# Gate logits with the tokens as the stationary operand: products turned around in a fused attention and mixture-of-experts kernel

## The chip, the cores and the metric

One core of one Trainium2 chip runs the whole program. The metric is device time in microseconds (us) of one execution. TensorE is called PE in the rows below (PEld are its weight loads), VectorE DVE, ScalarE ACT, GpSimd POOL, and SyncE, which issues most transfers, SP.

## The reference

Windowed attention with four sink positions runs over 4 batches and 8 heads of 768 positions with 64 channels; its output, laid out as 3072 tokens of 512 channels, goes through a mixture of 8 experts of which each token takes one. All arithmetic is in float32.

```python
scores = scale * np.matmul(q, k.transpose(0, 1, 3, 2))
keep = is_sink | in_window                      # 4 sinks, window of 128
scores = np.where(keep, scores, -1000000000.0)
a = np.exp(scores - np.max(scores, axis=-1, keepdims=True))
a = a / (np.sum(a, axis=-1, keepdims=True) + 1e-09)
x = np.matmul(a, v)                             # then tokens x 512 channels
logits = x @ w_gate                             # 512 x 8
e_idx = np.argmax(logits, axis=1)
gate_w = softmax(logits) at e_idx
eom = 1.0 / (1.0 + np.exp(-(x @ w_output_gate)))   # 512 x 8
out[mask] = gate_w * eom[:, e] * (np.maximum(x[mask] @ w1[e], 0.0) @ w2[e])
```

## The kernel before

**Attention by pairs.** Two neighbouring heads make a pair, `pair(p)` with p from 0 to 15, four pairs to a batch. For each of six blocks of 128 queries, PE forms the scores in 64x64 tiles (`score`, L1232) in a PSUM tile `s`, DVE folds the window and takes the maximum (`fold`, L1239 to L1244), and ACT takes the exponentials (`exps`, L1248) into `e`. There are two `s` tiles, so the third block of scores waits for the exponentials of the first. PE turns `e` over (`trans`, L1272), ACT copies that to `f` (L1275), POOL cuts the triangles (L367), and PE multiplies by the values in 64x64 tiles (`av`, L1335; the sinks in `av_sink`, L1357) into two PSUM tiles, `oA` for even blocks and `oB` for odd ones. Each exists once, so the next pair's first `av` waits until the last reader of this pair's `oA` and `oB` is done. ACT copies both to `ot` (L1363), which has channels on its partitions and tokens along its rows, not yet divided by the sums of the exponentials `rs`. `norm` (L1411, L1414) turns `ot` over, divides, and writes `x`, which is stored to `xd` in HBM.

**The gate, before.** `gate1` (L1370) holds the gate weights `wgt` (128 channels x 32: 16 columns for each head of the pair) as the stationary operand and streams the 128 tokens of a block past it, six products in 128x32 tiles; the logits come out with the 32 columns on partitions, in the fourth quarter of `oA` and `oB`. ACT copies them to `lgT` (L1375), PE turns them over with two transposes in a tile of the family `tp` (`gate2`, L1381; there are two `tp` tiles, which every turning shares), DVE multiplies by the reciprocals in `rs` (`weigh`, L1385) into `lw`, and POOL (DVE for the last two pairs) adds the heads into `lg` (L1393, L1395). After a batch's last pair, `gate_route` chooses each token's expert, counts (L546, L548) and sorts the tokens into a table: six PE products (`sort`, L610) and an addition on DVE (L613).

**The experts.** Four early slots (256 tokens of the commonest experts so far) can begin before attention ends; after the fourth batch's table, `final_table` splits what is left into 13 slots, each one expert's share of up to 384 tokens. A slot gathers its tokens (L890), turns them over (L950), splits them into a high part `xh` (ACT) and a low part `xl` (DVE, L955), and multiplies by both layers' weights (L1055 in the first early slot; L1074 and L1087, first layer; L1112, second layer), three products for each where the weights are split too. A half megabyte of weights is loaded into one of four `raw` tiles; ACT makes the high part (L925) and DVE the low part (L929, 1024 wide).

**What sets the order.** Nothing is written in the order in which it runs. Each step is given to a planner (`Plan.op`) with its engine, costs, tiles and a due time made of `AT` and `PAIR * p` (for a slot of `SLOT0 + STEP * k`), and for some steps overridden by `PIN`, a table by step number. `Plan.order` puts the steps of each engine in line, the engines then run in that order, and a step whose input is late holds up what stands behind it.

```python
pl.op("PE", fn=gate1, r=["wgt", (ot, 0), (ot, 1)], w=[oA, oB], at=(at, "g1"), **pe(450, "quad"))
pl.op("PE", fn=gate2, r=[(lgT, 0), (lgT, 1)], w=[gt], at=(at, "g2"), **pe(170))
pl.op("DVE", fn=weigh, r=[gt, (rs, "r")], w=[lw], at=(at, "lw"), **dve(192))
```

## Time and profile before

| what | value |
|---|---|
| median of 3 runs | 514.02 us (513.76 to 514.71) |
| profiled execution, its own time | 513.68 us |
| span of its instructions | 511.9 us |
| PE busy | 486.7 us (95%) |
| PE's weight loads busy | 384.0 us (75%) |
| DVE, ACT, POOL busy | 335.1, 285.0, 196.1 us |
| mean granted clock | 0.991 |

The span is what the instructions of the profiled execution cover; its own time is 1.8 us more. A PE that is busy in the rows is not one at its peak: products overlap, and the end of each is modelled. In the trace each float32 product stands as two records (six products of `gate1` are 12 records), so rows count records. All times in rows are from the start of the span.

### The profile page before, as it was taken

What the parts mean: (1) busy time and instruction counts of PE and PEld (TensorE: products, weight loads), DVE (VectorE), ACT (ScalarE), POOL (GpSimd) and SP (SyncE); (2) the same over time, 40 slices, a digit from 0 to 9 for tenths busy, and PEclk for the clock granted to TensorE, in tenths of its full rate; (3) what the DMA queues carried; (4) which work ended last, traced back from release to release, by engine and by line L of the source; (5) the groups of instructions that cost most, each with busy time, mean ns of one, the idle gap of its engine ahead of it and who ended that gap; (6) DMA issues with size and microseconds to landing.
All of it is one profiled execution on the core that took longest, in us unless ns stands there. A gap on an engine that the chain in (4) does not pass through costs nothing.

```text
span 511.9 us, 12956 instructions
## 1 busy us (share of the span) xinstructions
PE 486.7 (95%) x4797; PEld 384.0 (75%) x4797; DVE 335.1 (65%) x776; ACT 285.0 (56%) x773; POOL 196.1 (38%) x314
## 2 busy tenths in 40 slices
PE   8799989999999999999799999999999999999992
PEld 3467667766567884998799989989866878878872
DVE  4677897799856498899898621543636866275430
ACT  4788878878866525844446332534537856363430
POOL 7777778886882224231155023021133211000020
PEclk9999999999999999999899999999999999999997
DMA  8455653758961445974838449483898889986460
GB/s 302 128 168 153 216 161 124 233 166 297 388 187 40 155 131 201 315 258 146 294 101 314 148 153 343 156 293 90 282 363 319 283 289 310 367 266 230 141 260 21
DMA packets 61402, 112.52 MB, mean 220 GB/s; under 512 B 8076, under 2 KB 27664, under 8 KB 61330
## 3 DMA queue, kind: packets, MB, share of 16 engines
q1 hardware_dynamic: 56866, 97.47, 56.6%
q0 software_dynamic: 4464, 14.14, 7.9%
q8 instruction: 40, 0.66, 0.5%
q14 instruction: 32, 0.26, 0.1%
HBM read 98.41 MB, written 13.44 MB: 219 GB/s over the span
## 4 chain that ended last, share of the span: by engine, by line
PE 56%; issue 16%; DVE 12%; DMA 7%; ACT 5%; POOL 2%; another core or an unknown queue 0%; POOLq 0%; ACTq 0%; DVEq 0%
PE s L1074 14%; PE oA L1112 9%; PE oB L1112 7%; DMA raw<-in_w_dram 7%; PE s L1232 6%; PE tp L1272 3%; PE s L1055 3%; PE oA L1335 3%; PE oB L1335 2%; ACT e L1248 2%; PE tp L1411 2%; PE s L1087 2%; DVE nmx L1244 2%; DVE s L1241 1%; POOL out_dram L968 1%
## 5 line engine op out<-in xcount | busy, mean ns | idle before, releaser
L1248 ACT ACTIVATE e<-s,nmx 128x132 f32<-128x132 f32 x192 | 69.7, 371 | 28.5 <-DVE nmx L1244 24.6
L968 POOL DMA_INDIRECT out_dram<-y,idx x20 | 21.7, 1087 | 108.3 <-ACT y L965 94.4
L890 POOL DMA_INDIRECT xg<-xd,idx x21 | 24.5, 1168 | 93.3 <-PE tp L950 77.9
L986 ACT ACTIVATE hh<-s 128x512 fp32r<-128x512 f32 (+1 forms) x36 | 23.2, 644 | 64.3 <-PE s L1074 64.0
L1232 PE MATMUL s<-k,q 64*64 64x196 f32 (+1 forms) x768 | 51.8, 341 | 6.6 <-ACT e L1248 6.1
L989 DVE SCALAR_TENSOR_TENSOR hl<-s,hh 128x512 fp32r<-128x512 f32 (+1 forms) x36 | 26.8, 747 | 41.9 <-ACT hh L986 41.9
L1241 DVE COPY_PREDICATED s<-maskf,s 128x256 f32<-128x256 int32 x80 | 33.9, 424 | 15.9 <-PE s L1232 13.8
L1244 DVE TENSOR_REDUCE nmx<-s 128x2 f32<-128x264 f32 x96 | 41.5, 432 | 3.3
L1232 PEld LDWEIGHTS s<-k,q 64*64 64x64 f32 x768 | 23.3, 133 | 26.0 <-ACT e L1248 15.7
L1211 POOL TENSOR_SCALAR q<-q 128x256 f32<-128x256 f32 x45 | 37.9, 855 | 5.8 <-DMA q<-in_qT_dram 3.7
L1248 ACT ACTIVATION_READ_ACCUMULATOR e<-s,nmx 128x1 f32 x192 | 38.8, 202 | 0.0
L367 POOL TENSOR_SCALAR_AFFINE_SELECT g<-f 128x512 f32<-128x512 f32 (+1 forms) x48 | 27.6, 576 | 24.5 <-ACT f L1275 24.5
L1335 PE MATMUL oB<-g,v 64*64 64x128 f32 (+1 forms) x384 | 32.0, 248 | 0.2 <-ACT tick L1348 0.2
L1272 PE MATMUL tp<-ident,e 128*128 128x128 f32 x192 | 30.3, 282 | 1.7 <-DVE x L1414 0.8
L1275 ACT COPY f<-tp 128x512 f32<-128x512 f32 x48 | 28.1, 593 | 6.4 <-PE tp L1272 4.3
L1335 PE MATMUL oB<-f,v 64*64 64x64 f32 (+1 forms) x384 | 31.0, 244 | 0.0
L1335 PE MATMUL oA<-f,v 64*64 64x128 f32 (+1 forms) x384 | 30.6, 251 | 0.3 <-POOL f L367 0.3
L367 POOL TENSOR_SCALAR_AFFINE_SELECT f<-f 128x512 f32<-128x512 f32 (+1 forms) x48 | 27.0, 562 | 3.3
L1272 PEld LDWEIGHTS tp<-ident,e 128*128 128x128 f32 x192 | 20.8, 141 | 9.3 <-issue 2.4
L968 POOL DMA_INDIRECT out_dram<-y,idx_e x8 | 10.8, 1354 | 40.7 <-ACT y L965 39.4
L965 ACT ACTIVATE y<-oA,sc 128x512 f32<-128x512 f32 (+1 forms) x18 | 11.7, 651 | 23.6 <-PE oA L1112 18.0
L1335 PEld LDWEIGHTS oB<-g,v 64*64 64x64 f32 x384 | 23.0, 133 | 2.1 <-issue 1.0
(563 smaller groups left out, 1596.5 us busy)
## 6 DMA issues: line engine op xcount, KB each, us to landing
raw<-in_w_dram SPq DMA_DIRECT2D x96, 512.0 KB
v<-in_vx_dram SPq DMA_DIRECT2D x8, 768.0 KB
xd<-x SPq DMA_DIRECT2D x16, 384.0 KB
k<-in_kx_dram SPq DMA_DIRECT2D x15, 396.0 KB
q<-in_qT_dram SPq DMA_DIRECT2D x15, 384.0 KB
wa0h<-in_w_dram SPq DMA_DIRECT2D x2, 512.0 KB
wa0l<-in_w_dram SPq DMA_DIRECT2D x2, 512.0 KB
wa1h<-in_w_dram SPq DMA_DIRECT2D x2, 512.0 KB
```

The source lines that it names most:

```text
L367: nc.gpsimd.affine_select(out=ap, in_=ap if src is None else src, pattern=pattern, compare_op=op, fill=fill, base=base, channel_multiplier=cm)
L968: nc.gpsimd.indirect_dma_start(out=where, out_offset=bass.IndirectOffsetOnAxis(ap=ids(), axis=0), in_=p.get(yk)[:, 0:m], in_offset=None, b ...
L1074: nc.tensor.matmul(out=p.get(ps)[:, j, 0:cols], lhsT=a, rhs=p.get(x)[:, d, 0:cols], start=d == 0 and i == 0, stop=d == ND - 1 and i == 2)
L1112: nc.tensor.matmul(out=p.get(ys[s]), lhsT=h[a][:, s * P:(s + 1) * P], rhs=w[b_], start=f == 0 and i == 0, stop=f == NF - 1 and i == len(th ...
L1211: (nc.gpsimd if p else nc.vector).tensor_scalar(out=c, in0=c, scalar1=SCALE, scalar2=None, op0=ALU.mult)
L1232: nc.tensor.matmul(out=get(s)[h * D:(h + 1) * D, a, c0:c1], lhsT=get(q)[r, t * P + h * D:t * P + (h + 1) * D], rhs=get(k)[r, k0 + c0 - o0: ...
L1241: nc.vector.copy_predicated(out=both[:, :, 4:CW], mask=bc(maski[:, 1, 4:CW], 1, 2), data=z[:, :, 0:P])
L1244: nc.vector.tensor_reduce(out=get(nmx)[:, t, :], in_=both, axis=AX.X, op=ALU.max, negate=True)
L1248: nc.scalar.activation(out=get(e)[:, t, a, :], in_=get(s)[:, a, P:P + CW], func=AF.Exp, bias=get(nmx)[:, t, a:a + 1], scale=1.0, accum_out ...
L1272: nc.tensor.transpose(out=get(tp)[:, i, :], in_=get(e)[:, 2 * j + i // 2, i % 2, 4:CW], identity=ident)
L1275: nc.scalar.copy(out=get(f)[:, two].rearrange("p t a r -> p (t a) r"), in_=get(tp))
L1335: nc.tensor.matmul(out=o, lhsT=get(v)[rows_, kt, p % 2 * P + a * D:p % 2 * P + (a + 1) * D], rhs=get((f, g)[src == "g"])[rows_, kt, a, c0: ...
```

## The change

The gate's products are turned around. In `gate`, a 64x64 piece of `ot` (64 channels of one head x 64 tokens) is the stationary operand, and that head's 16 columns of `wgt` stream past it: 24 products for a pair (six blocks, two halves of the tokens, two heads), cycling through the four 64x64 tiles that the scores use. The logits come out with tokens on partitions, the even head's in `oA` and the odd head's in `oB`. The two ACT copies to `lgT` and the two transposes are gone, and with them one use of a `tp` tile. DVE weighs straight from `oA` and `oB`, in two instructions of 96 columns where there was one of 192; they, and no longer ACT, are the last readers of `oA` and `oB`. The planner's numbers (`SOFT`, `SLOT0`, `AT`, `PIN`) are new throughout, so all engines run in another order. The amount of work outside the gate is the same.

```diff
-SOFT = 12779
-SLOT0, STEP, PLAIN, FSTEP = 196777, 20000, 1, 800
+SOFT = 13716
+SLOT0, STEP, PLAIN, FSTEP = 196911, 20000, 1, 800
...
-    12: -24621, 50: 3844, 52: 25562, 59: -91499, 60: -90999, 61: -91498, 66: -14940, 68: 18874, 69: 19874, 71: 18872,
+    12: -24621, 18: 2353, 21: 1853, 24: 10220, 35: 64141, 36: 1854, 44: 4741, 50: 5428, 51: 64641, 52: 26563,
...
-            lgT = new(pl, "lgT", [96, 2, P], key=("lgT", p))
-
-            def gate1():
-                for i, o in enumerate((oA, oB)):
-                    for j in range(3):
-                        nc.tensor.matmul(out=get(o)[32 * j:32 * j + 32, 3, :], lhsT=wgt[:, hp, :], rhs=get(ot)[:, 3 * i + j, :],
-                                         start=True, stop=True, skip_group_check=True)
-
-            pl.op("PE", fn=gate1, r=["wgt", (ot, 0), (ot, 1)], w=[oA, oB], at=(at, "g1"), **pe(450, "quad"))
-            for i, o in enumerate((oA, oB)):
-                pl.op("ACT", fn=lambda i=i, o=o: nc.scalar.copy(out=get(lgT)[:, i, :], in_=get(o)[0:96, 3, :]), r=[o], w=[(lgT, i)], at=(at, "lgT"), **act(128))
-            gt, lw = new(pl, "tp", [P, 4, P]), new(pl, "lw", [P, T, 2, 2 * E])
-
-            def gate2():
-                lr = get(gt).rearrange("p a q -> p (a q)")[:, 0:2 * 96]
-                for a in range(2):
-                    nc.tensor.transpose(out=lr[:, a * 96:(a + 1) * 96], in_=get(lgT)[:, a, :], identity=ident[0:96, 0:96])
-
-            def weigh():
-                lr = get(gt).rearrange("p a q -> p (a q)")[:, 0:2 * 96]
-                tt(out=get(lw), in0=lr.rearrange("p (t a e) -> p t a e", t=T, a=2), in1=bc(get(rs), 3, 2 * E), op=ALU.mult)
+            def gate():
+                for t in range(T):
+                    for h in range(2):
+                        for a, o in enumerate((oA, oB)):
+                            r = slice(a * D, (a + 1) * D)
+                            nc.tensor.matmul(out=get(o)[h * D:(h + 1) * D, 3, t * 2 * E:(t + 1) * 2 * E], lhsT=get(ot)[r, t, h * D:(h + 1) * D],
+                                             rhs=wgt[r, hp, a * 2 * E:(a + 1) * 2 * E], start=True, stop=True, skip_group_check=True)
+
+            pl.op("PE", fn=gate, r=["wgt", (ot, 0), (ot, 1)], w=[oA, oB], at=(at, "g1"), **pe(550, "four"))
+            lw = new(pl, "lw", [P, T, 2, 2 * E])
+
+            def weigh(a, o):
+                def fn():
+                    tt(out=get(lw)[:, :, a, :], in0=get(o)[:, 3, 0:T * 2 * E].rearrange("p (t e) -> p t e", t=T),
+                       in1=bc(get(rs)[:, :, a], 2, 2 * E), op=ALU.mult)
+                return fn
...
-            pl.op("PE", fn=gate2, r=[(lgT, 0), (lgT, 1)], w=[gt], at=(at, "g2"), **pe(170))
-            pl.op("DVE", fn=weigh, r=[gt, (rs, "r")], w=[lw], at=(at, "lw"), **dve(192))
+                pl.op(name, fn=fn, r=[(lw, 0), (lw, 1)] if hp == 0 else [(lw, a)], w=[lg], at=(at, "add"), **cost)
+
+            for i, o in enumerate((oA, oB)):
+                pl.op("DVE", fn=weigh(i, o), r=[o, (rs, "r")], w=[(lw, i)], at=(at, "lw"), **dve(96))
```

The order of PE around the first pair's gate, before (tiles by their names, with numbers where there are several; the last column is the shape of the output and how many equal products follow each other; line numbers of after are 17 higher around the attention):

```order
L1303 MATMUL tp_555<-ident,pk_541 24x128 x2
L1370 MATMUL oA<-ot_545,wgt 32x128 x3
L1370 MATMUL oB<-ot_545,wgt 32x128 x3
L1411 MATMUL tp_573<-ident,ot_545 128x128 x4
L1411 MATMUL tp_578<-ident,ot_545 128x128 x2
L1232 MATMUL s_212<-k_234,q_229 64x196 x4
L1232 MATMUL s_209<-k_234,q_229 64x196 x4
L1381 MATMUL tp_604<-ident,lgT_592 128x96 x2
L1272 MATMUL tp_607<-ident,e_530 128x128 x4
```

The same place after, with the first two of the 24 products (the other 22 alternate between `oA` and `oB` in the same way):

```order
L1423 MATMUL tp_549<-ident,ot_526 128x128 x4
L1387 MATMUL oA<-wgt,ot_526 64x16
L1387 MATMUL oB<-wgt,ot_526 64x16
...
L1249 MATMUL s_212<-k_234,q_229 64x196 x4
L1320 MATMUL tp_591<-ident,pk_535 24x128 x2
L1423 MATMUL tp_599<-ident,ot_526 128x128 x2
L1249 MATMUL s_209<-k_234,q_229 64x196 x4
```

The gate now stands next to a block of scores, which has the same 64x64 tiles, and nothing of it comes back to PE later. Counted from the first instruction to the last pair's gate, PE goes from one tile shape to another 153 times in the order of before (128-wide, 64x64, or the gate's 128x32) and 124 times in that of after.

SP's first transfers, before (`q_207` and `k_219` are the first pair's, in two parts each; `v_221` holds the values of the first two pairs):

```order
L1191 DMA q_207<-in_qT_dram 128x256
L1191 DMA k_219<-in_kx_dram 128x264
L1196 DMA v_221<-in_vx_dram 128x6x256
L1191 DMA q_207<-in_qT_dram 128x512
L1191 DMA k_219<-in_kx_dram 128x528
```

And after:

```order
L1208 DMA q_207<-in_qT_dram 128x256
L1208 DMA k_219<-in_kx_dram 128x264
L1208 DMA q_207<-in_qT_dram 128x512
L1208 DMA k_219<-in_kx_dram 128x528
L1213 DMA v_223<-in_vx_dram 128x6x256
```

The values now come behind the rest of the first pair's queries and keys.

PE at the products of the last batch's table, before (`xg_3631` and `xg_3638` are the fourth early slot's two tiles of tokens; the two rows of `L610` stand six times):

```order
L1112 MATMUL oB<-wb1l,hh_4090 128x512
L1112 MATMUL oB<-wb1h,hl_4098 128x512
L950 MATMUL tp_4198<-ident,xg_3631 128x128 x4
L950 MATMUL tp_4206<-ident,xg_3638 128x128 x4
L610 LDWEIGHTS ohrow
L610 MATMUL tp_4233<-rhs,ohrow 128x256
...
L1074 MATMUL s_212<-xh_4211,wb2h 128x256
L1074 MATMUL s_212<-xl_4217,wb2h 128x256
```

And after (the fourth early slot's tokens are `xg_3890` and `xg_3898`):

```order
L1091 MATMUL s_209<-xl_4034,wa2h 128x256
L1091 MATMUL s_209<-xh_4026,wa2l 128x256
L627 LDWEIGHTS ohrow
L627 MATMUL tp_4299<-rhs,ohrow 128x256
...
L967 MATMUL tp_4309<-ident,xg_3890 128x128 x4
L1129 MATMUL oA<-wa3h,hh_4118 128x512
L1129 MATMUL oA<-wa3l,hh_4118 128x512
```

The table's products were right behind two turnings that fill both `tp` tiles; now they are ahead of them, behind first-layer products. Between the last pair's gate and these products stand 112 second-layer products before and 64 after, and 144 first-layer products in both; on DVE, 24 low parts of weights (L929) stand between the last weighing and the table's addition before, and 16 after.

## Rows read from the trace of the kernel before

**Rows 1.** The page: busy us of each engine, share of the span, instructions.
```profile
PE 486.7 (95%) x4797; PEld 384.0 (75%) x4797; DVE 335.1 (65%) x776; ACT 285.0 (56%) x773; POOL 196.1 (38%) x314
```

**Rows 2.** Stages: length, busy time (instructions) by engine, clock, DMA share, GB/s.
```profile
120.00:135.00 15.00, 14.05 (x202) 8.72 (x194) 13.45 (x37) 12.76 (x56) 14.09 (x25) 1.00 1.03 388
...
300.00:350.00 50.00, 50.00 (x284) 45.21 (x283) 19.22 (x20) 19.46 (x29) 9.97 (x10) 1.00 0.64 219
...
400.00:450.00 50.00, 48.43 (x305) 40.95 (x304) 31.24 (x36) 29.16 (x40) 7.38 (x6) 1.00 0.90 311
```

**Rows 3.** The same view in stretches of 5 us, around 250 us.
```profile
245.00:250.00 5.00, 2.20 (x19) 1.82 (x18) 4.51 (x12) 4.46 (x7) 1.90 (x2) 0.97 0.91 303
250.00:255.00 5.00, 5.00 (x32) 5.00 (x32) 3.44 (x16) 0.60 (x2) 0.46 (x1) 0.68 0.92 307
```

**Rows 4.** Waits: who waited for whom, us in total, times, longest.
```profile
PE s L1232 <- ACT e L1248: 6.1, 12, 1.7
PE tp L610 <- DVE xl L955: 2.8, 1, 2.8
...
PEld s L1232 <- issue: 3.6, 18, 0.4
```

**Rows 5.** Timeline of PE around one gate: start, us, instructions in order.
```profile
97.80 0.39 PE L1381 MATMUL tp<-ident,lgT 96*128 96x96 f32 x2
98.11 0.56 PE L1232 MATMUL s<-k,q 64*64 64x196 f32 x8
98.50 0.22 PE L1335 MATMUL oB<-g,v 64*64 64x64 f32 x1
...
101.16 0.66 PE L1272 MATMUL tp<-ident,e 128*128 128x128 f32 x4
101.65 0.38 PE L1303 MATMUL tp<-ident,pk 128*24 128x128 f32 x2
101.97 0.56 PE L1232 MATMUL s<-k,q 64*64 64x196 f32 x8
102.46 0.42 PE L1370 MATMUL oA<-ot,wgt 128*32 128x128 f32 x6
...
103.03 0.87 PE L1411 MATMUL tp<-ident,ot 128*128 128x128 f32 x6
103.83 0.56 PE L1232 MATMUL s<-k,q 64*64 64x196 f32 x8
```

**Rows 6.** Timeline of PE in the products with the values: the first records of two successive rounds.
```profile
96.90 0.22 PE L1335 MATMUL oA<-g,v 64*64 64x64 f32 x1
...
96.96 0.22 PE L1335 MATMUL oA<-g,v 64*64 64x64 f32 x1
```

**Rows 7.** Single lines: shortest, median, longest ns of the instructions of each.
```profile
L1375 ACT COPY lgT<-oA x16: 237/258/296, 28.9 to 189.7; 96x128 f32<-96x128 f32 x16
L1385 DVE TENSOR_TENSOR lw<-tp,rs x16: 294/348/358, 30.9 to 191.0; 128x192 f32<-128x192 f32 x16
L1395 DVE TENSOR_TENSOR lg<-lg,lw x4: 251/255/259, 167.3 to 191.8; 128x96 f32<-128x96 f32 x4
```

**Rows 8.** Timeline of the start: start, us, instruction, idle time before it.
```profile
5.85 2.65 PE L1170 MATMUL oB<-ones 128*128 128x512 bf16 x8
...
7.70 0.50 DVE L1211 TENSOR_SCALAR q<-q 128x256 f32<-128x256 f32 x2 [0.34 <-DMA q<-in_qT_dram]
...
10.18 0.37 ACT L1248 ACTIVATE e<-s,nmx 128x132 f32<-128x132 f32 x1 [1.91 <-DVE nmx L1244]
```

**Rows 9.** Timeline at the last batch's table.
```profile
248.93 0.83 PE L610 MATMUL tp<-rhs,ohrow 128*128 128x256 bf16 x6 [2.80 <-DVE xl L955]
```

**Rows 10.** The chain that ended last, in order of time: one piece of the experts' stage.
```profile
259.82 0.69 PE oA L1112 x3
```

**Rows 11.** The page, costliest groups: busy us, mean ns of one, idle before.
```profile
L1241 DVE COPY_PREDICATED s<-maskf,s 128x256 f32<-128x256 int32 x80 | 33.9, 424 | 15.9 <-PE s L1232 13.8
L1244 DVE TENSOR_REDUCE nmx<-s 128x2 f32<-128x264 f32 x96 | 41.5, 432 | 3.3
```

More of the change, by code (lines that the diff above doesn't have):

```diff
@@ L50 @@
 PAIR, RAT = 9500, 17500
-SOFT = 12779
-SLOT0, STEP, PLAIN, FSTEP = 196777, 20000, 1, 800
+SOFT = 13716
+SLOT0, STEP, PLAIN, FSTEP = 196911, 20000, 1, 800
 AT = {
-    "load": -118603, "v": -35855, "vs": 192361, "scale0": 15699, "scale1": -134944, "scale2": 109581, "s0": 1473,
-    "s1": 6371, "s2": 9983, "s3": 9722, "s4": 5928, "s5": 7612, "fold": -35886, "exp": 26303, "tr0": 16369,
-    "tr1": 43278, "tr2": 48009, "trc": 44928, "mask": 28425, "guard": -77108, "pack": -25682, "skT": 560,
[4 rows of a table removed]
+    "load": -118732, "v": -30065, "vs": 176077, "scale0": 13546, "scale1": -120030, "scale2": 117104, "s0": 1505,
+    "s1": 5879, "s2": 10225, "s3": 8686, "s4": 3321, "s5": 8000, "fold": -37670, "exp": 39128, "tr0": 15004,
+    "tr1": 41717, "tr2": 52343, "trc": 61586, "mask": 27001, "guard": -75245, "pack": -23336, "skT": 8752,
[4 rows of a table added]
 }
 PIN = {
[49 rows of a table removed]
[66 rows of a table added]
 }
@@ L1145, in moe_kernel @@
         for fam, n, pool in (("q", 3, "qk"), ("k", 3, "qk"), ("e", 2, "qk"), ("v", 2, "bp"), ("x", 2, "bp"),
-                             ("f", 2, "bp"), ("g", 2, "bp"), ("pk", 2, "bp"), ("hlk", 2, "bp"), ("ot", 2, "bp"), ("tick", 2, "bp"), ("lgT", 2, "bp"),
+                             ("f", 2, "bp"), ("g", 2, "bp"), ("pk", 2, "bp"), ("hlk", 2, "bp"), ("ot", 2, "bp"), ("tick", 2, "bp"),
                              ("lw", 2, "bp"), ("lg", 2, "bp"), ("nmx", 2, "bp"), ("rs", 4, "bp"),
@@ L1395, in fn @@
                         eng.tensor_tensor(out=get(lg), in0=get(lg), in1=w[:, :, a, :], op=ALU.add)
-                pl.op(name, fn=fn, r=[lw], w=[lg], at=(at, "add"), **cost)
-            pl.op("PE", fn=gate2, r=[(lgT, 0), (lgT, 1)], w=[gt], at=(at, "g2"), **pe(170))
-            pl.op("DVE", fn=weigh, r=[gt, (rs, "r")], w=[lw], at=(at, "lw"), **dve(192))
+                pl.op(name, fn=fn, r=[(lw, 0), (lw, 1)] if hp == 0 else [(lw, a)], w=[lg], at=(at, "add"), **cost)
+            for i, o in enumerate((oA, oB)):
+                pl.op("DVE", fn=weigh(i, o), r=[o, (rs, "r")], w=[(lw, i)], at=(at, "lw"), **dve(96))
             for a in range(2 if hp else 1):
@@ L1455, in moe_kernel @@
         on = {fam: [i for x in pl.inst.values() if x["fam"] == fam for i in x["users"]]
-              for fam in ("q", "k", "e", "v", "x", "f", "g", "pk", "hlk", "tick", "ot", "lgT", "lw", "lg", "nmx", "rs")}
+              for fam in ("q", "k", "e", "v", "x", "f", "g", "pk", "hlk", "tick", "ot", "lw", "lg", "nmx", "rs")}
         def close_q():
```

121 rows, old and new, of tables (AT, PIN) are left out of this document.

## Prediction

> **What bounds the kernel now.** I read the page first. PE is busy for 486.7 of 511.9 us, 95%, and no other engine for more than 65% [rows 1]. So the first question for each part of the change is what it does to PE's time. The stages then show that "PE-bound" means two things. From 300 us on PE is busy in every slice (50.00 of 50 us), while DVE and ACT have more than half of their time free [rows 2]. There products follow at a steady pace, three second-layer products in 0.69 us [rows 10], and a microsecond that PE gains earlier stays gained as long as the weights arrive. In the attention stage PE, DVE and POOL are all at about 90% (14.05, 13.45 and 14.09 of 15 us in the slice at 120 us, ACT 12.76, [rows 2]). That is a loop, scores to maximum to exponentials to the next scores, rather than one full engine. The waits say the same: what PE waits for most is ACT's exponentials, which give back the tile of scores, 6.1 us in 12 waits, and the only other large one is a single wait of 2.8 us ahead of a table's products [rows 4].
>
> That single wait is the third thing to see. In the slice 245 to 250 us PE works for 2.20 of 5 us, and in the next slice the granted clock is 0.68 [rows 3], a part of it at the lower level of 1.2 GHz instead of 2.4 GHz. The timeline shows why PE stood still: the products of the last batch's table (L610) need a `tp` tile, both had just been filled by the turnings of the fourth early slot, and DVE freed one only with its second `xl` at 248.9 us [rows 9].
>
> **The products of the gate.** Before, a gate of 12 records takes 0.57 us from its start to that of the next block (102.46 to 103.03), and the two transposes back 0.31 us (97.80 to 98.11) [rows 5]. Each figure holds one change of tile shape at its end. What that is worth shows in the same rows: eight records of scores take 0.39 us when 64x64 products follow (98.11 to 98.50) and 0.49 when another shape does (101.97 to 102.46), so 0.10 us. Six turnings ahead of scores take 0.80 us (103.03 to 103.83), where four ahead of another turning take 0.49, or 0.735 for six, so 0.065 us. With 0.10 us taken off, the gate costs 0.47 and the transposes 0.21, together 0.68 us a pair.
>
> After, there are 24 products, 48 records. The trace has no product of 16 columns. The nearest row is that of the products with the values: four records of 64 columns in four tiles every 0.06 us (96.90 and 96.96 [rows 6]). At that pace twelve rounds take 0.72 us, the upper bound. If the pace followed the streamed columns alone, a round of 16 columns would take a quarter, and the gate 0.18 us, the lower bound. I take 0.60, near the upper end, because the stationary piece that each product loads is as large as in those rows and only the streamed part shrinks. That is 0.08 us less than 0.68 for each of 16 pairs: **-1.3 us**, between -8.0 and +0.6.
>
> The Trainium skill, "TensorEngine Tiling (Array Packing)", section on instruction overhead, warns against this: a matmul has about 60 cycles of overhead, one of a single column takes as long as one of 60, and a dimension that is already small should not be divided further. By its figure 48 records in a row would be an estimated 1.2 us. The rows above, with a record every 15 ns on average, agree with it only if the overheads of four tiles overlap; then its estimate is 0.3 us.
>
> **Changes of tile shape.** The order of PE up to the last gate has 153 before and 124 after, 29 fewer, since the gate now has the scores' shape. At 0.10 us each that is **-2.9 us**. The ends are 0.065 us (-1.9) and the 0.2 us for which weight loads sit with nothing to wait for ahead of a block of scores (3.6 us in 18 times [rows 4]; -5.8).
>
> **ACT and DVE.** ACT loses two copies a pair, 0.258 and 0.268 us [rows 7], 8.4 us in all. ACT is not full, so this is not 8.4 us of time; it helps where PE waits for exponentials that queue behind such a copy. I give it **-1.0 us** of those 6.1, between 0 and -3. DVE's one weighing of 0.348 us becomes two of 96 columns; the nearest row, an addition of 128x96, takes 0.255 [rows 7]. So DVE does 0.16 us more a pair, 2.6 us in all, which I cost at nothing: in the fullest slice it has 1.5 of 15 us free [rows 2], and there it needs 0.3. If that cover were gone it would cost up to 2.6 us. The additions to `lg` are the same, on the same engines, and stand off PE's path.
>
> **The start.** The values now load behind the rest of the first pair's queries. Before, PE fills 2.65 us with idle products (5.85 us on), DVE's scaling at 7.70 us waits for the transfer of `q`, and ACT stands still for 1.91 us until 10.18 [rows 8]. The transfer that is moved back has 128x6x256 float32, 786 kB; at the 388 GB/s of the fullest slice [rows 2] it takes 2.0 us. So the first pair's later scores can start up to 2 us sooner, but the second pair's queries still come behind the same bytes. I take **-1.0 us**, between 0 and -1.9.
>
> **The wait at the table.** The table's products now stand ahead of the fourth slot's turnings, so the `tp` tiles are not both taken just before. PE comes to them with 48 second-layer products less behind it since the last gate, 11.0 us at 0.23 each [rows 10]; on DVE eight low parts of weights have gone from ahead of the table, so both sides come sooner. I let the 2.8 us go [rows 4], and with it the clock: 0.32 of 5 us, 1.6 us [rows 3]. Together **-4.4 us**, with 0 as the other end.
>
> **What a new order brings.** Every engine's order is another, and I cannot read from it which waits appear. PE's waits for exponentials, 6.1 us, are the measure of what one order has of them. I add half of it, **+3.0 us**, between 0 and +6.
>
> **Sum.** -1.3 - 2.9 - 1.0 - 1.0 - 4.4 + 3.0 = -7.6 us on the profiled execution's 513.68: 506.1. Its time is 0.3 us under the median of the runs shown, so I predict **506.5 us** for the median. The part after 300 us moves forward as a whole.
>
> **Rivals.** (1) The main case: the gain arrives, 503 to 509.5 us. Chance 0.48.
>
> (2) The wait at the table, or one as long, stays somewhere, with its fall of the clock. The term of 4.4 us falls away: 510.9. For it: DVE is 90% busy in 245 to 250 us as well [rows 3], and the table hangs on DVE. Against it: what held up PE was a tile, and that cause is gone. Chance 0.20.
>
> (3) The gain is given back later. Between 400 and 450 us the DMA engines are busy for 0.90 of the time and PE idles for 1.6 us [rows 2]. If the loads of weights there, and not PE, set the pace, then starting sooner changes little: 513 to 514. Against it: between 300 and 350 the share is 0.64, so loads have room to run ahead. Chance 0.12.
>
> (4) Slower: `oA` and `oB`, of which there is one each, are now released by DVE, and the next pair's first product with the values waits for that. What queues behind it on PE is the next block of scores. If DVE's second weighing comes one step of folding and maximum late, 0.42 and 0.43 us [rows 11], all 16 pairs lose 13.7 us: 520. It decides from 0.48 us a pair on, which uses up the 7.6 us. For it: DVE is 90% busy in this stage. Against it: in the order after, scores, turnings or `norm` stand between a gate and the next pair's values. Chance 0.12.
>
> (5) Slower: the 48 records don't overlap. Four turnings of 128 columns take 0.49 us for eight records, 0.061 us a record [rows 5]; with loads of half that width 0.03 us, so 1.47 us a pair, 0.87 more than I took, 13.9 us: 520. [rows 6] speak against it. It is the case that the Trainium skill's overhead per matmul describes, if the four tiles did not hide it. Chance 0.05.
>
> The last 0.03 is for waits of other kinds that add up to more than the gain.
>
> **How the numbers follow.** 0.2% of this kernel, 1.0 us, is about what a measurement can tell from no change. Faster: (1), (2) and a third of (3), 0.71. Same: most of the rest of (3), 0.09. Slower: (4), (5) and the rest, 0.20. The range takes in (1), (2) and (3), 0.80 of the chance: from 502.5, which is the sum with shape changes at their upper price, to 514.5. The main case alone reaches from 503 to 509.5.
>
> **What would show it.** Each gate should be 48 records of 64x64 in about 0.6 us from its start to the next block's; 0.8 or more would make the first step wrong. The idle time of PE up to 30 us should be shorter by about 1 us. The last pair's weighing, at 191.0 us before [rows 7], should come 4 to 6 us sooner. Ahead of the last table's products there should be no wait over 1 us, and no slice between 230 and 270 us at a clock under 0.95. From 300 us on PE should stay full. The prediction is wrong if PE waits for DVE's weighing ahead of the values in most pairs, if a new wait of several microseconds stands between 180 and 260 us, or if PE idles behind weights between 370 and 470 us.

## The result

The changed kernel is slower. Its median is 518.47 us (515.37 to 522.24, 17 runs) beside 514.71 us (511.79 to 518.65, 17 runs) of the kernel before in the same job; the ratio is 1.0077, interval 1.005 to 1.0104. The forecast was 506.5 us. Ratios leave out executions that took over 1.5% longer than the fastest of their kernel.

The page of the changed kernel, in the form of [rows 1]. Its lines are 17 higher than before in the functions ahead of the gate (L1232 is now L1249), and the gate is L1387, the weighing L1395.

```profile
PE 485.1 (94%) x5341; PEld 389.8 (76%) x5341; DVE 334.5 (65%) x792; ACT 279.6 (54%) x741; POOL 193.3 (37%) x314
```

PE has 1.6 us less to do, ACT 5.4 us less, and yet the span is 515.9 us, 4.0 more. So the question is where PE stands still. Stretches of 5 us show it, and with them the two later stages of [rows 2]; the first row is the kernel before.

```profile
15.00:20.00 5.00, 2.75 (x37) 1.12 (x35) 4.29 (x18) 3.39 (x15) 3.52 (x8) 1.00 0.55 175
```

```profile
15.00:20.00 5.00, 2.58 (x41) 1.71 (x43) 3.87 (x17) 2.94 (x14) 3.42 (x8) 0.88 0.44 140
20.00:25.00 5.00, 5.00 (x112) 4.38 (x108) 1.70 (x5) 2.75 (x11) 3.69 (x6) 0.77 0.11 39
120.00:125.00 5.00, 2.22 (x30) 1.28 (x34) 4.49 (x12) 3.47 (x16) 3.68 (x7) 0.97 1.00 346
125.00:130.00 5.00, 5.00 (x118) 4.49 (x114) 2.78 (x8) 2.75 (x13) 2.50 (x5) 0.69 1.08 387
245.00:250.00 5.00, 5.00 (x24) 4.05 (x23) 5.00 (x8) 2.40 (x3) 0.00 (x0) 1.00 0.60 215
250.00:255.00 5.00, 4.26 (x23) 3.40 (x22) 4.85 (x11) 2.10 (x2) 1.58 (x2) 1.00 0.48 154
300.00:350.00 50.00, 50.00 (x275) 44.87 (x274) 19.16 (x20) 18.78 (x29) 9.90 (x10) 1.00 0.68 240
400.00:450.00 50.00, 50.00 (x305) 44.35 (x304) 30.80 (x35) 27.90 (x40) 5.72 (x5) 1.00 0.87 306
```

The hole at 245 us of [rows 3] and the clock of 0.68 behind it are gone, and from 300 us on PE is full. In the attention stage PE works for about half of the time in two stretches, 15 to 20 and 120 to 125 us, and behind each the granted clock falls to 1.2 GHz for a part of the next stretch (0.77 and 0.69). Only the second is new: the kernel before has the first as well (2.75 of 5 us), in this profile with its clock at 1.00. The waits of PE, in the form of [rows 4], name what PE stood still for: the exponentials.

```profile
PE s L1249 <- ACT e L1265: 9.7, 12, 2.3
PE s L1091 <- DVE xl L972: 1.7, 2, 1.0
...
PE tp L967 <- DVE tab L630: 0.8, 1, 0.8
```

A gate in the timeline, as in [rows 5] (first records of the first, the last two rounds, and the next block):

```profile
28.22 0.23 PE L1387 MATMUL oA<-wgt,ot 64*64 64x16 f32 x1
...
28.82 0.21 PE L1387 MATMUL oA<-wgt,ot 64*64 64x16 f32 x1
...
28.88 0.21 PE L1387 MATMUL oA<-wgt,ot 64*64 64x16 f32 x1
...
28.94 0.54 PE L1249 MATMUL s<-k,q 64*64 64x196 f32 x8
```

Twelve rounds at 0.06 us, 0.72 us in all: the upper bound of the prediction, the pace of [rows 6] in spite of the streamed part being a quarter. The weighings, in the form of [rows 7], with what DVE waited for ahead of them:

```profile
L1395 DVE TENSOR_TENSOR lw<-oA,rs x16: 245/248/259, 29.2 to 195.8; 128x96 f32<-128x96 f32 x16
L1395 DVE TENSOR_TENSOR lw<-oB,rs x16: 193/246/258, 29.4 to 195.7; 128x96 f32<-128x96 f32 x16
...
  PE oB L1387: 7.7, 5
```

Only 2.1 of these 7.7 us lie before 165 us, in the stage in which PE waits for exponentials.

### The profile page after: what moved, and what is told of

It is laid out like the page before. It is cut to its first block, busy times and chain, and to the rows that moved or that the text cites. A ratio compares the mean times of both kernels' runs of the same rounds, so it can differ in the third digit from the quotient of the medians.

```text
span 515.9 us, 14061 instructions
## 1 busy us (share of the span) xinstructions
PE 485.1 (94%) x5341; PEld 389.8 (76%) x5341; DVE 334.5 (65%) x792; ACT 279.6 (54%) x741; POOL 193.3 (37%) x314
## 4 chain that ended last, share of the span: by engine, by line
PE 54%; issue 14%; DVE 12%; DMA 12%; ACT 4%; POOL 2%; SPq 0%; another core or an unknown queue 0%; POOLq 0%; ACTq 0%; DVEq 0%
PE s L1091 15%; PE oA L1129 9%; DMA raw<-in_w_dram 6%; PE s L1249 5%; PE oB L1129 5%; PE tp L1289 3%; PE s L1072 3%; PE oA L1352 3%; PE oB L1352 2%; ACT e L1265 2%; PE s L1104 2%; PE tp L1423 2%; DVE s L1258 1%; DVE nmx L1261 1%; DMA xg<-xd,idx_e 1%
## 5 line engine op out<-in xcount | busy, mean ns | idle before, releaser
L1249 PE MATMUL s<-k,q 64*64 64x196 f32 (+1 forms) x768 | 52.6, 344 | 11.3 <-ACT e L1265 9.7
L1249 PEld LDWEIGHTS s<-k,q 64*64 64x64 f32 x768 | 22.8, 135 | 29.1 <-ACT e L1265 20.8
L1352 PE MATMUL oB<-g,v 64*64 64x128 f32 (+1 forms) x384 | 33.3, 256 | 0.0
L1289 PE MATMUL tp<-ident,e 128*128 128x128 f32 x192 | 31.5, 286 | 1.7 <-issue 1.1
L1352 PE MATMUL oA<-f,v 64*64 64x128 f32 (+1 forms) x384 | 32.0, 259 | 0.7 <-issue 0.7
L1289 PEld LDWEIGHTS tp<-ident,e 128*128 128x128 f32 x192 | 21.3, 143 | 11.1 <-issue 4.4
L616 POOL TENSOR_TENSOR rhs<-oh,ohj 128x512 bf16<-128x512 bf16 x12 | 13.8, 1162 | 38.2 <-DVE ohj L602 21.9
L1352 PEld LDWEIGHTS oB<-g,v 64*64 64x64 f32 x384 | 24.6, 139 | 1.0 <-issue 0.3
L1352 PEld LDWEIGHTS oA<-f,v 64*64 64x64 f32 x384 | 23.6, 139 | 1.5 <-issue 0.8
```

Of the source, the lines that this page charges most:

```text
L1249: nc.tensor.matmul(out=get(s)[h * D:(h + 1) * D, a, c0:c1], lhsT=get(q)[r, t * P + h * D:t * P + (h + 1) * D], rhs=get(k)[r, k0 + c0 - o0: ...
L1289: nc.tensor.transpose(out=get(tp)[:, i, :], in_=get(e)[:, 2 * j + i // 2, i % 2, 4:CW], identity=ident)
L1352: nc.tensor.matmul(out=o, lhsT=get(v)[rows_, kt, p % 2 * P + a * D:p % 2 * P + (a + 1) * D], rhs=get((f, g)[src == "g"])[rows_, kt, a, c0: ...
```

## The experiments

All ratios are to the kernel before, run in the same job. First a second look at the kernel before, since two executions of one kernel differ.

**The kernel before once more.** No edit.

> The kernel before once more, for its trace alone. If the falls of the clock belong to the order: one, near 249 us, as in the first profile, and time within 1 us of it. If they come by chance of the execution (the one-step change of the table showed falls at 21 and 69 us in an order that is the same as before up to there): one to three falls, others than in the first profile, and a time that differs by about 1.7 us for each.

Its time was 514.63 us, its span 512.8. Clock by stretches:

```profile
20.00:25.00 5.00, 5.00 (x86) 3.66 (x89) 1.57 (x4) 2.58 (x11) 3.27 (x6) 0.66 0.02 5
...
70.00:75.00 5.00, 5.00 (x126) 4.32 (x122) 3.78 (x13) 3.30 (x14) 1.90 (x4) 0.82 0.45 157
...
250.00:255.00 5.00, 3.10 (x18) 3.04 (x19) 4.86 (x15) 3.07 (x5) 2.27 (x2) 0.77 0.86 271
```

The same program, in the same order, fell to the lower clock three times where the first profile shows one fall, near 250 us. That is as in the second expectation, but the time isn't: with two falls more it is 0.95 us longer and not 3.4. So a fall that stands in one profile and not in another is not by itself an effect of the change, and this profile is the fairer partner of the changed kernel: both have two falls up to the last gate. Its last gate starts at 191.07 us, not 189.23: 1.84 us later with the two falls. Now the span can be cut at the start of the last gate. The rows are the kernel before (second profile), then the changed kernel; PE's busy time is the number behind the length.

```profile
0.00:191.07 191.07, 180.04 (x3016) 128.54 (x3016) 140.56 (x408) 133.76 (x551) 130.84 (x258) 0.98 0.57 188
191.07:512.80 321.73, 308.49 (x1782) 257.71 (x1781) 193.83 (x369) 150.79 (x222) 65.02 (x56) 0.99 0.69 238
```

```profile
0.00:194.61 194.61, 177.97 (x3527) 133.15 (x3527) 140.65 (x425) 129.10 (x521) 129.99 (x258) 0.98 0.57 187
194.61:515.90 321.29, 307.10 (x1816) 256.67 (x1815) 193.88 (x367) 150.48 (x220) 63.34 (x57) 0.99 0.69 237
```

Up to the last gate PE is busy for 2.07 us less (177.97 - 180.04) and idle for 5.61 us more (16.64 - 11.03): 3.54 us late. More than half of this idle time, 3.0 us, lies between 30 and 100 us and not at the two stretches above (the second profile of before, then the changed kernel):

```profile
30.00:100.00 70.00, 67.36 (x1299) 49.20 (x1295) 54.70 (x149) 55.72 (x243) 55.01 (x103) 0.98 0.53 171
```

```profile
30.00:100.00 70.00, 64.37 (x1515) 47.95 (x1515) 53.98 (x155) 52.98 (x224) 51.84 (x99) 1.00 0.51 161
```

Behind the last gate the changed kernel is 0.44 us faster. That is a gain and a loss, which the last product of PE and POOL's last branch tell apart (again before, then changed; POOLq is POOL's sequencer, and its rows have the number of instructions, their ns, and the start of the first and the last):

```profile
503.32 0.40 PE L1112 MATMUL oA<-wa0h,hl 128*128 128x512 f32 x1
...
L1647 POOLq EVENT_SEMAPHORE  x3: 17/17/17, 505.3 to 505.5; - x3
...
L1647 POOLq COMPARE_BRANCH  x1: 45/45/45, 504.9 to 504.9; - x1
```

```profile
504.34 0.40 PE L1129 MATMUL oA<-wa0h,hl 128*128 128x512 f32 x1
...
L1659 POOLq EVENT_SEMAPHORE  x3: 17/17/17, 508.7 to 508.9; - x3
...
L1659 POOLq COMPARE_BRANCH  x1: 45/45/45, 505.9 to 505.9; - x1
```

PE's last product ends at 503.72 us before and at 504.74 after, 1.0 us late, so 2.5 of the 3.54 us are made good by then. From there to the end of the span it is 9.1 us before (in both profiles) and 11.2 after: POOL goes on 0.4 us behind its branch before and 2.8 us behind it after. So of the 3.1 us between the two spans, 1.0 is what PE loses in the attention stage less what it gains behind it, and 2.0 stand at the end of the program, behind all products. The long end isn't tied to the gate's form: it is 11.1 to 11.4 us where only the amount of gate work or three routing steps of the changed kernel differ, 11.5 and 11.6 with the old gate in the two remade orders below, and 9.2 with the new gate in the fourth. What makes it is open.

**Each gate in the other's order.** The order is written out as a list of steps in place of the planner's choice; the first kernel has the new gate in the order of before, the second the old gate in the order of the changed kernel.

```diff
-            for e, xs in ready.items():
...
+        todo = list(FIXED)
...
+            for i in todo:
+                if i in ready[ops[i]["eng"]]:
...
+FIXED = (
...
```

> The new gate with everything else in the order of before: the order is written out as a list (FIXED) that follows before, the new products at the place of the old ones, the values loaded ahead again. Theory A (the new form of the gate saves some 2.6 us of PE's time and the newly made order loses 8.5 us in waits and falls of the clock): the waits of before come back, the saving stays, 511 to 513 us beside 514.7, ratio 0.993 to 0.997; one fall of the clock near 249 us, none before it. Theory B (the gate itself loses: 0.72 us of PE a pair, two weighings on DVE that hold oA and oB): as slow as the changed kernel, ratio 1.004 to 1.011.

> The old gate (with the copies on ACT and the transposes back) with everything else in the order of the changed kernel, the values loaded late as there. Theory A: the waits of the changed kernel, and the 2.6 us that the new gate saves are lost as well: 520 to 523 us, ratio 1.011 to 1.016; falls of the clock before 130 us. Theory B: the loss goes with the new gate, 511 to 515 us, ratio 0.992 to 1.001.

Both theories fell. The new gate in the old order took 526.71 us (1.0227, 1.0198 to 1.0257), the old gate in the new order 527.35 us (1.024, 1.021 to 1.027). Either half of the change by itself costs 12 to 13 us. PE's waits in the first of them:

```profile
PE s L1249 <- ACT e L1265: 5.9, 11, 1.7
PE oA L1352 <- DVE lw L1395: 5.6, 7, 1.4
```

The second row is the mechanism of the prediction's rival (4): the products with the values wait for the weighing. The rows of the changed kernel have no such wait; its order has weighings ahead of foldings instead. A third kernel tried to get both: the old order, and on DVE each weighing moved ahead to where the gate has just ended.

> The new gate in the order of before, as in the first experiment, but on DVE the two weighings stand ahead of the first folding and maximum that began, in the trace of before, when the gate's products had ended; they stood up to a whole block later there. Theory C (the gate in itself saves PE time, and what it needs is another order: values waited 5.6 us for weighings in the first experiment): that wait goes to under 1.5 us and what is behind it comes back, 512 to 517 us, ratio 0.996 to 1.005. Rival D (the 0.5 us of DVE a pair ahead of the foldings costs as much wherever it stands): scores wait for exponentials 9 us or more, ratio 1.010 to 1.023.

It took 522.78 us (1.0151, 1.0109 to 1.0193), a ratio of rival D, but only a part of its mechanism: the values' wait for weighings is gone, and scores wait for exponentials 7.6 us in 13 times and not 9.

**What a microsecond is worth.** Four kernels in the order of the changed one put work onto PE or DVE, or take it off.

```diff
-                for t in range(T):
+                for t in list(range(T)) * 2:
```

> The changed kernel, with the 48 records of each gate issued twice (the second time writes the same results), the order unchanged: 0.72 us of PE more in each of 16 pairs, 11.5 us in all. If PE's time sets the pace of the attention stage (which the prediction took for granted when it summed PE's microseconds): 11 to 12 us over the changed kernel, ratio to before 1.029 to 1.032. If the loop from scores to exponentials sets it, and PE has its waits to give: 3 to 6 us over the changed kernel, ratio 1.013 to 1.020.

```diff
-                    tt(out=get(lw)[:, :, a, :], in0=get(o)[:, 3, 0:T * 2 * E].rearrange("p (t e) -> p t e", t=T),
+                    for _ in range(2): tt(out=get(lw)[:, :, a, :], in0=get(o)[:, 3, 0:T * 2 * E].rearrange("p (t e) -> p t e", t=T),
```

> The changed kernel with each of the 32 weighings issued twice (the second writes the same values): 0.5 us of DVE more a pair, 8 us in all, the order unchanged. By the prediction, which cost DVE's added 0.16 us a pair at nothing since other work covers it: 0 to 2 us over the changed kernel, ratio to before 1.008 to 1.012. If DVE is on the path of the attention stage: 6 to 10 us over it, ratio 1.019 to 1.028, and then the added 0.16 us a pair has cost 2 to 3 us.

```diff
-                for t in range(T):
+                for t in range(T if p == 0 else T // 2):
```

> The changed kernel, its order unchanged, with half of the gate's products left out in 15 of 16 pairs (blocks 3 to 5 of the tokens; the weighing takes the logits of blocks 0 to 2 for them), 0.36 us of PE less a pair, 5.4 us in all. If a microsecond that PE gains in the attention stage reaches the end, as the prediction's sum took for granted: 5 to 6 us under the changed kernel, ratio to before 0.996 to 0.998. If DVE's chain sets the pace there: 0 to 2 us under it, ratio 1.004 to 1.008, and PE's waits grow by what it gains.

```diff
-            for i, o in enumerate((oA, oB)):
-                pl.op("DVE", fn=weigh(i, o), r=[o, (rs, "r")], w=[(lw, i)], at=(at, "lw"), **dve(96))
+            pl.op("DVE", fn=weigh, r=[oA, oB, (rs, "r")], w=[lw], at=(at, "lw"), **dve(192))
```

> The changed kernel with the two weighings of 96 columns as one of 192, at the place of the first (both heads' logits are taken from oA, oB's are left out, since one instruction can't read both tiles), the order otherwise unchanged: DVE 0.15 us less a pair, 2.3 us in all. Theory E (each microsecond of DVE there is one of the kernel, 8.6 us for 8.0 when the weighings were doubled): 2 to 3 us under the changed kernel, ratio to before 1.002 to 1.004. If DVE's added time is hidden, as the prediction had it: within 1 us of the changed kernel, ratio 1.006 to 1.010.

Measured: gate twice 534.41 us (1.0389, 1.0357 to 1.0421), weighing twice 527.12 us (1.0257, 1.0218 to 1.0296), half a gate 516.08 us (1.0018, 0.9988 to 1.0048), one weighing 529.1 us (1.0286). The last one's logits send tokens to other experts, so its end is another: PE is busy for 315.52 us behind the last gate, where the changed kernel has 307.10, and only the part up to the gate can be compared. Half a gate has other logits too, but as much work behind the gate (307.25 us). The rows, each cut at the start of its last gate: gate twice, weighing twice, half a gate, one weighing.

```profile
0.00:206.97 206.97, 189.47 (x4246) 144.63 (x4246) 142.16 (x425) 129.59 (x521) 130.51 (x258) 0.98 0.55 176
```

```profile
0.00:203.53 203.53, 184.04 (x3527) 135.79 (x3527) 149.09 (x455) 129.31 (x521) 130.22 (x258) 0.97 0.55 179
```

```profile
0.00:191.61 191.61, 172.79 (x3191) 126.79 (x3191) 140.50 (x425) 128.81 (x521) 130.25 (x258) 0.99 0.59 189
```

```profile
0.00:194.72 194.72, 178.32 (x3526) 132.84 (x3526) 141.10 (x410) 129.26 (x521) 130.27 (x258) 0.98 0.58 187
194.72:526.50 331.78, 315.52 (x1872) 260.62 (x1871) 194.38 (x367) 152.03 (x224) 66.39 (x58) 0.99 0.67 230
```

Work that is added costs at least itself: 11.5 us of PE (189.47 - 177.97) cost 15.9 us (534.41 - 518.47), more than either expectation, and 8.4 us of DVE (149.09 - 140.65) cost 8.7. The clock has a part in it: with the weighings twice PE has the same products and is busy for 6.1 us more (184.04 beside 177.97), at a mean clock of 0.97. Work that is taken off PE comes back in part: with half a gate PE was busy for 5.2 us less, the last gate came 3.0 us sooner, at a mean clock of 0.99 and not 0.98, and the median fell by 2.4, between the two expectations; by the two intervals it could be 1 to 5 us. One weighing for two was to take 16 times 0.14 us off DVE, but DVE's busy time up to the last gate did not fall (141.10 beside 140.65), nor did the gate come sooner (194.72 beside 194.61), so this run says little. It seems that no engine alone sets the pace of this stage. Neither PE's products nor DVE's weighings explain the loss by their length.

**The largest wait of the changed kernel.** It is ahead of scores at 124.39 us. The timeline around it:

```profile
120.79 0.75 DVE L593 RECIPROCAL denw<-den 128x96 f32<-128x96 f32 x1
...
121.46 1.17 DVE L608 TENSOR_TENSOR ohrow<-io,jf 128x768 bf16<-128x768 f32 x1
...
122.55 0.42 DVE L1258 COPY_PREDICATED s<-maskf,s 128x256 f32<-128x256 int32 x1
...
123.00 0.43 DVE L1261 TENSOR_REDUCE nmx<-s 128x2 f32<-128x264 f32 x1
...
123.52 0.37 ACT L1265 ACTIVATE e<-s,nmx 128x132 f32<-128x132 f32 x1 [1.45 <-DVE nmx L1261]
...
124.39 0.73 PE L1249 MATMUL s<-k,q 64*64 64x196 f32 x8 [2.28 <-ACT e L1265]
```

Read from the bottom: PE waits 2.28 us for exponentials, ACT 1.45 us for a maximum, and DVE was at routing steps of the second batch from 120.79 to 122.55 us, ahead of that folding. The experiment moves these steps behind foldings (rows of DVE's order, + is the experiment):

```
 L1258 COPY_PREDICATED s_212<-maskf,s_212 128x2x128
 L1261 TENSOR_REDUCE nmx_2335<-s_212 128x2
+L1258 COPY_PREDICATED s_209<-maskf,s_209 128x2x128
+L1261 TENSOR_REDUCE nmx_2335<-s_209 128x2
...
 L593 RECIPROCAL denw<-den 128x96
...
 L608 TENSOR_TENSOR ohrow<-io_97,jf 128x768
 L1258 COPY_PREDICATED s_209<-maskf,s_209 128x2x128
-L1261 TENSOR_REDUCE nmx_2335<-s_209 128x2
```

> The changed kernel with three routing steps of the second batch (L608, L593 and the one between them) moved on DVE behind one to four foldings that they stood ahead of (place 122 us). If that is what made the wait of 2.28 us ahead of scores: the wait is under 1 us and the fall of the clock behind it goes in most executions, 1.5 to 3.5 us less than the changed kernel, ratio to before 1.001 to 1.005. If the wait only moves on to what now stands behind those steps: within 1 us of the changed kernel, ratio 1.006 to 1.010.

518.12 us, 1.0073 (1.0046 to 1.01): no change. The wait shrank from 2.28 to 1.17 us, the clock still falls behind it (0.67 in 125 to 130 us), and the last gate starts at 194.84 us: up to there PE is idle for 0.4 us less (16.23 beside 16.64) and busy for 0.6 us more (178.61 beside 177.97). So half of this wait was worth nothing in the end; what the whole of it is worth isn't shown.

**The table's wait alone.** The kernel before, with the last batch's table products ahead of the fourth early slot's turnings, as in the changed kernel (PE's order; on DVE the table's addition moves ahead with them):

```
+L610 MATMUL tp_4168<-rhs,ohrow 128x256
...
 L1112 MATMUL oB<-wb1h,hl_4098 128x512
 L950 MATMUL tp<-ident,xg 128x128 x4
 L950 MATMUL tp<-ident,xg 128x128 x4
-L610 MATMUL tp_4233<-rhs,ohrow 128x256
```

> The kernel before with one step moved: the last batch's table products (L610) stand ahead of the fourth early slot's two turnings and not behind them, as in the changed kernel. By the prediction's term the wait of 2.8 us at 246 us and the fall of the clock behind it go, and nothing takes their place: 4.4 us less, ratio 0.991 to 0.993. If the wait only moves on (to the turnings, or to DVE's steps behind them): 0 to 1.5 us less, ratio 0.997 to 1.000, and a gap of over 1 us or a fall of the clock within 10 us of the old place.

516.0 us, ratio 1.002 (0.9993 to 1.0047): no gain. In its profile the part behind the last gate is 321.15 us beside 321.73, and the clock is 0.85 and 0.81 in the two stretches from 250 to 260 us, as in the second expectation. The timeline of PE at the old place:

```profile
249.80 0.60 PE L950 MATMUL tp<-ident,xg 128*128 128x128 f32 x4
251.09 0.66 PE L950 MATMUL tp<-ident,xg 128*128 128x128 f32 x4 [0.69 <-DVE tab L613]
252.42 0.38 PE L1074 MATMUL s<-xh,wb2h 128*128 128x256 f32 x1 [0.68 <-ACT xh L953]
253.95 0.58 PE L1074 MATMUL s<-xl,wb2h 128*128 128x256 f32 x1 [1.15 <-DVE xl L955]
```

Three waits of 2.52 us in all stand where one of 2.80 us stood [rows 9]: for the table's addition that frees the tile, for the high part, for the low part. All three are for DVE or ACT, and another order of PE did not shorten them. The changed kernel has waits of the same kind, 1.7 us for low parts and 0.8 for the table's addition, but no fall of the clock there (1.00 from 245 to 255 us).

**Another form of the gate.** Tokens stationary in whole 128x128 tiles, logits straight into a `tp` tile, one weighing; `oA` and `oB` come free with ACT's copies.

```diff
+                for t in range(T):
+                    nc.tensor.matmul(out=lr[:, t * 32:(t + 1) * 32], lhsT=get(ot)[:, t, :], rhs=wgt[:, hp, :],
+                                     start=True, stop=True, skip_group_check=True)
```

> Another form of the turned gate in the order of before: tokens stationary in whole 128x128 tiles, six products of 32 columns into a tile of turnings (tp), at the place where the transposes back stood; oA and oB come free with ACT's copies of the values, and DVE weighs once, 192 columns as before. Theory E (the changed kernel loses through DVE, which works 0.15 us a pair more and has to weigh before oA and oB come free; neither is so here, and ACT's copies are saved all the same): 508 to 513 us, ratio 0.988 to 0.998, PE waits for nothing that hangs on a weighing. Rival F (an order made for the durations of before loses with any other gate, as in the first and the weigh-early experiment): ratio 1.005 to 1.020.

> The gate in whole 128x128 tiles into a tile of turnings, one weighing, as in the old order, but in the order of the changed kernel, at the place of its gate and of its first weighing, the values loaded late. If the newly made order costs by itself (theory A's part that is left): 3 to 8 us over the same gate in the old order, ratio to before 1.002 to 1.012. If the loss lay in the gate's form alone: within 1.5 us of it.

531.87 us (1.0318, 1.0283 to 1.0352) in the old order and 538.92 us (1.0456, 1.0417 to 1.0494) in the new one. Here the price was misjudged:

```profile
129.43 1.52 PE L1385 MATMUL tp<-wgt,ot 128*128 128x32 f32 x12
130.79 0.41 PE L1289 MATMUL tp<-ident,e 128*128 128x128 f32 x2
```

A gate of this form takes 1.36 us of PE (129.43 to 130.79), 0.113 us for each of 12 records, nearly twice the 0.72 of the 64x64 form. With some 0.6 us a pair more on PE the two runs cannot tell theory E from its rival. The new order costs 7.1 us over the old one with this gate, within the 3 to 8 us expected if a newly made order costs by itself; but neither order was made for this gate.

**Orders made anew.** For each form of the gate two orders of all engines up to pair 14 were made alike, by exchanging steps and adding up durations taken from the traces, and then two more for the new gate that reach beyond the last gate. In the first four only the list `FIXED` differs; in the last two, tiles of a family are also taken in the turn in which they came free.

> The changed kernel's gate, with the order of all engines up to the gate of pair 14 made anew (written out as a list; from there on as in the changed kernel). Theory G (the waits of the attention stage belong to the order, and an order made for this gate can shorten them): last gate at 184 to 191 us and not 194.6, 506 to 515 us, ratio 0.985 to 1.000. Rival H (the new gate, which holds oA and oB until DVE has weighed, makes the waits in any order): 517 us or more, ratio 1.004 to 1.02.

> The gate of before, with the order up to the gate of pair 14 made anew in the same way as for the new gate. If orders hold both forms back: 507 to 513 us, ratio 0.985 to 0.997. The new gate's saving of PE time (2 to 3 us up to the last gate, by the two kernels' busy times) should leave it 0 to 3 us behind the new gate in its remade order; if the new form costs by itself (rival H), it is 2 us or more ahead of it.

> As the first of these, another order made in the same way: tells how much two such orders differ. Theory G: 506 to 515 us, ratio 0.985 to 1.000, within 4 us of the first. Rival H: 517 us or more.

> As the second, the old gate in another order made in the same way: 507 to 515 us, ratio 0.985 to 1.000, within 4 us of the first order with this gate; 0 to 3 us behind the mean of the two orders with the new gate if the new form saves, 2 us or more ahead of it if it costs.

> The changed kernel's gate, all engines' order remade up to and beyond the last gate, starting from the changed kernel's order; tiles of a family are taken in the turn in which they came free. Theory G (the order had the loss): last gate at 182 to 190 us, no PE wait over 1.5 us between 30 and 190 us, 503 to 512 us, ratio 0.978 to 0.996. Rival H (the new form makes waits in any order): last gate at 192 us or later, ratio 1.000 to 1.015.

> The same, starting from the first remade order. Theory G: 503 to 512 us, ratio 0.978 to 0.996, since what was ahead by 4 us at pair 13 stays ahead. Rival H: level with or behind the first remade order, ratio 1.000 to 1.015.

| gate | order | median us | ratio to before |
|---|---|---|---|
| new | remade, first | 515.51 | 1.0014 (0.9987 to 1.004) |
| new | remade, second | 525.88 | 1.0221 (1.0174 to 1.0269) |
| new | third | 534.28 | 1.043 (1.0363 to 1.0497) |
| new | fourth | 529.57 | 1.0265 (1.018 to 1.0351) |
| old | remade, first | 537.11 | 1.0407 (1.0361 to 1.0453) |
| old | remade, second | 531.62 | 1.0321 (1.0283 to 1.0358) |

PE's waits in the first of them:

```profile
PE s L1249 <- ACT e L1265: 2.3, 6, 0.6
PE tp L1423 <- DVE x L1426: 1.9, 1, 1.9
PE tp L1289 <- issue: 1.9, 1, 1.9
```

Its part up to the last gate, and the same up to the gate of pair 13:

```profile
0.00:194.52 194.52, 179.71 (x3526) 129.52 (x3527) 140.77 (x425) 130.39 (x521) 130.08 (x258) 0.99 0.61 187
```

```profile
0.00:156.10 156.10, 143.45 (x3057) 99.24 (x3057) 120.11 (x362) 113.59 (x479) 120.10 (x242) 1.00 0.61 188
```

With the same gate and the same work, the waits for exponentials are 2.3 us here and 9.7 us in the changed kernel. The gate of pair 13 starts at 156.10 us and not at 160.21, without a fall of the clock; behind it one of the two waits of 1.9 us (at 162.19 us) and a fall (0.78 in 165 to 170 us), near where the remade part joins the old rest, take that back in this execution (194.52 beside 194.61). By the medians the kernel is level with before, and its interval lies below that of the changed kernel. Its executions also have the higher clock, 0.987 to 0.994 beside 0.979 to 0.988. So rival H is wrong for this order, and some 0.6% of the loss (1.0077 to 1.0014) belongs to the order. But theory G's gain did not come either: one order in four reached 1.00, none went below, the last two, meant to move the joint away, were slower, and the eight orders of the new gate lie between 515.5 and 534.3 us. The old gate fared worse in orders made in the same way (531.6 and 537.1; in the slower of them PE stands still once for 7.4 us, at 199.75 us); two against two, with 5 to 10 us between orders of one gate, that shows only that the new form is not the dearer one by more than orders differ.

## Why the prediction was wrong

By its own steps, against the second profile of before (512.8 us), which has as many falls of the clock up to the last gate as the profile after. Forecast were -7.6 us, measured +3.1.

**The gate's products**, forecast -1.3 us: 0.72 us a pair for 0.68, +0.6. The pace is the upper bound, that of [rows 6], so the streamed columns don't set it; that the loads of the stationary pieces do is not shown. By the Trainium skill, "TensorEngine Tiling (Array Packing)", section on instruction overhead, the estimates were 0.3 us with four overlapping tiles and 1.2 us without; the trace, at 0.72, lies between.

**Changes of tile shape**, -2.9: PE's busy time up to the last gate fell by 2.07 us in all; with the +0.6 of the gate that leaves -2.7. As a remainder this agrees, but no run shows that it comes from the tile shapes: with the new gate in the old order PE is busy for 182.59 us up to the last gate, 2.6 us more than before, at the same mean clock (0.98).

**ACT's relief (-1.0), the start (-1.0) and the new order (+3.0)**, together +1.0: PE's idle time up to the last gate rose by 5.6 us. This is the step that failed most. ACT does have 4.7 us less to do there (129.10 beside 133.76; 5.4 on the page, not the 8.4 of the copies' durations), but PE's waits for exponentials rose from 6.1 [rows 4] to 9.7 us; the other 2.0 us are smaller waits of several kinds. The first gate starts at 28.22 us beside 28.34 in the second profile, so the start brought 0.1, and PE's idle time up to 30 us, which was to fall by 1 us, rose from 5.3 to 6.2. The last pair's weighing, said to come 4 to 6 us sooner than 191.0 us, comes 4.7 us later. And the new order cost nearly the whole of the range that it was given. The waits for exponentials come and go with the order: 9.7 us here, 2.3 in the first remade order with the same gate.

**The wait at the table**, -4.4: up to PE's last product the part behind the last gate became 2.5 us shorter. The wait itself went, as forecast, and the fall of the clock with it (PE is busy for 1.4 us less there), but PE's idle time fell by only 1.1 us, since smaller waits of 3.0 us in all stand behind the last gate now. In the run with this step alone the 2.8 us reappear as 2.5 us in three pieces.

**The end of the program** had no term; "the part after 300 us moves forward as a whole". It cost 2.0 us behind PE's last product.

The five corrections are 1.9, 0.2, 4.6, 1.9 and 2.0 us; -7.6 and 10.6 make +3.0, the measured 3.1 but for rounding.

**What lay under the largest** was the way of summing: the prediction read from [rows 2] that the attention stage is a loop of engines at 90%, and then added PE's microseconds as if they reached the end. That row is the fullest slice; between 30 and 100 us PE was busy for 96% and DVE, ACT and POOL for 78 to 80% (67.36, 54.70, 55.72 and 55.01 of 70 us), which is still a loop without much room. Half a gate suggests that PE's microseconds are worth about half there, and the doubled gate and weighing that a microsecond more costs 1.0 to 1.4. In these runs a saving was in part lost in the next wait, and a loss was not.

**Readings that were off.** PE is not busy throughout from 300 us on: it has 48.43 of 50 us between 400 and 450 us, where DVE and ACT are busy for over half [rows 2]. Rival (5) counted the four turnings of [rows 5] as eight records; the row has four (x4), 0.12 us each, so its price would be some 37 us and not 13.9. The sum with shape changes at their upper price is 503.6 and not 502.5.

**The rivals.** (4) had the right sign and a real mechanism at the wrong place: values wait for weighings in the old order (5.6 us), not in the new one. (2) had a part: waits stay at the table, but none as long, and no fall of the clock. (5) is refuted by the rounds of 0.06 us, (3) by PE's full stretches from 300 us on. DVE's 0.16 us a pair, costed at nothing, does not show in DVE's busy time up to the last gate (140.65 us beside 140.56); what its weighings cost in waits is not shown, though as an addition they do cost (weighing twice).

**What stays open.** Whether some order makes the new gate faster than the kernel before; the best of those run draws level. Which of the many exchanges between the two orders makes the 7.4 us of waits for exponentials; halving the largest single wait brought nothing. And why POOL stands still behind its last branch in some of these programs.

## What to carry to other kernels

Where several engines in a loop are nearly full, price a change from both sides: here a microsecond saved on PE brought about half of itself, one that was added cost 1.0 to 1.4, and the waits of a new order were the largest term with the widest range. Before a wait is counted as gone, look at what else is late there: if the engine that released it is full, a part of the wait moves on to the next thing it makes. A new form of a step and the order around it are one change; each alone lost 12 to 13 us here, so neither can be judged by swapping it in. And follow the span to its end: two of the three microseconds stood behind the last product.

## What the hardware showed unexpectedly

The same program, in the same order, fell to 1.2 GHz once in one execution and three times in another while PE had work left, and the last gate came 1.84 us later in the second. A product with a 128x128 float32 stationary piece and 32 streamed columns takes 0.113 us a record, while four records with 64x64 pieces and 16 columns take 0.06 us together, as long as with 64 columns: a quarter of the streamed columns did not make these products cheaper. And the end of the program, behind the last product, took 9.1 us in some of these programs and 11.2 in others, with POOL's step behind a branch 0.4 or 2.8 us away.
